# One hundred and eleven tasks at other positions in a hand-kept order of a two-stage kernel

## The chip, the cores and the metric

The kernel runs on one core of a Trainium2 chip. The core has a tensor engine (PE, with its weight loads listed as PEld), a vector engine (DVE), a scalar engine (ACT), GpSimd (POOL, idle here) and a sync engine (SP) that issues the DMAs. Each engine takes its own instructions in order, and semaphores hold an instruction until what it needs is there. The metric is the device time of one execution in microseconds (us).

## The reference

Attention with positive random features over 8 batches, 8 heads, 576 tokens and a head width of 64, and then a feed-forward layer with the activation g = h tanh(softplus(h)) on the 4608 tokens of width 512:

```python
def phi(x):
    proj = np.einsum('bhsd,df->bhsf', x, w_phi)                  # 64 -> 128 features
    proj = proj - np.max(np.abs(proj), axis=-1, keepdims=True)
    return np.concatenate([np.exp(proj), np.exp(-proj)], axis=-1)
q_p, k_p = phi(q), phi(k)
kv  = np.einsum('bhsf,bhsd->bhfd', k_p, v)
z   = np.sum(k_p, axis=2)
num = np.einsum('bhsf,bhfd->bhsd', q_p, kv)
den = np.einsum('bhsf,bhf->bhs', q_p, z)[..., None] + 1e-06
x   = (num / den)            # transposed to 4608 x 512
h   = x @ w_in               # 512 -> 2048
sp  = np.where(h > 20.0, h, np.log1p(np.exp(np.minimum(h, 20.0))))
out = (h * np.tanh(sp)) @ w_out                                  # 2048 -> 512
```

## The kernel before

All work is cut into 3160 small tasks, each on one engine with a name, and the names are used in this document.

Attention. "project k15" or "project q5_0" multiplies 512 columns of keys or queries by w_phi into two PSUM banks, pp0 and pp1 (eight matmuls, in turn to pp0 and pp1, line 422). "centre" on DVE takes the largest magnitude of each (line 426) and subtracts it (line 434): up to k16 and q5_1 one task of four instructions (maximum of pp0, maximum of pp1, subtraction of pp0, subtraction of pp1), later four tasks, "max" and "centre" with 0 and 1. "exp" on ACT makes both exponentials. "sum k15 13" adds a block of keys into the product with v of pair 13 in PSUM, "kv 13" copies it out (on DVE or ACT), "num q5_0 0" multiplies queries by it, "divide" on DVE divides by the denominator, and the result is turned (by PE early, by a DMA round trip with "regroup" on DVE later) and split into a high and a low part ("high", "low").

Feed-forward. A chunk c has 256 tokens; "in c f" multiplies its x by 128 columns of w_in (12 matmuls of fp32r: high by high, high by low, low by high, line 660) into half of a PSUM bank h; when both halves (f even and f odd) are there, "mish" on ACT reads the bank. "out c f" multiplies by w_out (lines 695 and 830). From chunk 4 on, "mix", "mixh", "mixl" build sums of the activations and the out products run on sums of weights (tasks "wsum", "comb", "combh", "combl", "send", made once, between about 180 and 300 us) with seven instead of eight products. The weights themselves are split into two parts early, by "abs", "clamp", "shift", "sign", "rest", "power", "split" and "ready".

Banks. PSUM has three pools: "att" with four buffers, "h" with two and "o" with two. The bank of "in c f" is of pool "h". From k15 on, a projection's pp0 is of pool "h" too and its pp1 of pool "att". A new tile waits until the last reader of the tile that had its buffer is done.

Order. `Plan.order` is a list scheduler with due times. Its result goes through `relinked`, which moves single tasks on their engine's own line by the list MOVES: a pair (name, ahead) puts the task directly ahead of another one on the same engine. The lines of the four engines are then merged into one program order by needs. What stands first on an engine is done first there; a task that waits holds up all behind it.

Of the kernel before, what the change touches and what calls it, by code (L numbers as in the profile page):

```python
# [87 lines left out]
BURST = ("share", "sum", "num", "project")  # L88
PATIENCE = 1.451

MOVES = (("rest ('in', 2, 2)", "low 1 2"), ("low 1 1", "sign ('in', 2, 1)"),
# [7 lines left out]


def relinked(tasks):

    by_name = {task["name"]: task for task in tasks}
    line, at = {}, {task["name"]: n for n, task in enumerate(tasks)}
    for task in tasks:
        line.setdefault(task["engine"], []).append(task["name"])
    for name, ahead in MOVES:
        own = line[by_name[name]["engine"]]
        own.remove(name)
        own.insert(own.index(ahead), name)  # L110
    needs, then, key = dict.fromkeys(at, 0), {name: [] for name in at}, {}
    for task in tasks:
        for need in {*task["deps"], *task["after"]}:
            needs[task["name"]] += 1
            then[need].append(task["name"])
    for own in line.values():
        first = len(tasks)
        for one, two in zip(own, own[1:]):
            needs[two] += 1
            then[one].append(two)  # L120
        for name in reversed(own):
            first = key[name] = min(first, at[name])
    heap = sorted((key[name], at[name], name) for name in at if not needs[name])
    order = []
    while heap:
        name = heapq.heappop(heap)[2]
        order.append(by_name[name])
        for other in then[name]:
            needs[other] -= 1
            if not needs[other]:  # L130
                heapq.heappush(heap, (key[other], at[other], other))
    return order


class Plan:
# [11 lines left out]
    def order(self):  # L147
# [5 lines left out]
        done, slots, released, freed = {}, {}, {}, {}  # L153
# [27 lines left out]
        while any(waiting.values()):  # L181
            moved = False
            for engine, queue in waiting.items():
                if free[engine] > now or not queue:
                    continue
                found, held = None, engine == "PE" and last["kind"] in BURST and now > 190
                line = queue[:48]
# [39 lines left out]
                moved = True  # L227
# [5 lines left out]
        tasks = [task for _, _, task in issued]  # L233
        at = [n for n, task in enumerate(tasks) if task["name"].startswith("load ")][:NLOADS]
# [3 lines left out]
        moved = [next(task for task in tasks if task["name"] == name) for name in LATER]  # L238
        tasks = [task for task in tasks if task["name"] not in LATER]
        at = 1 + next(n for n, task in enumerate(tasks) if task["name"] == LATER_THAN)  # L240
        return relinked(tasks[:at] + moved + tasks[at:])


@with_exitstack
def attention_then_mish(ctx, tc, qT, kT, va, w_phi, w_in, w_out, out):
# [842 lines left out]
    def plan_fast(n, c, m):  # L1088
# [13 lines left out]
        for order, i in enumerate(by_use):  # L1102
            nth, kind = 4 * late + i, "kept" if i == 4 else "late" if c == NCH - 1 and late >= 0 else "ring"
            if kind == "kept" and c > FAST:
                continue
            if kind == "ring" and c > FAST and place < 2:
                ends.append(loaded[m % 2, i][1])
                continue
            r = 4 * (m % 2) + i if i < 4 else NFT // 2 + m
            slot, token, after = f"hs{r}", f"hs:{key} {i}", []  # L1110
            deps = [plain_out(FAST - 1, r), f"wsum {r // 2} {r % 2}"]
            if kind == "ring":
                if (m % 2, i) in loaded:
                    deps, after = [], [loaded[m % 2, i][0]]
                loaded[m % 2, i] = f"term {key} {i}", token
                if c == NCH - 1 or place < NFT // 2 - 2:
                    ends.append(token)
            elif kind == "late":
                slot, token, deps = "e", f"late:{nth // 2}", []
                after = [f"term {key} {i ^ 1}"] if i in (0, 2) else []  # L1120
            add(f"term {key} {i}", "SP", n + 0.5 + LAGF - TLEAD + 0.1 * order, 0.42, lambda i=i: load_term(c, m, i),
                deps=deps + [f"send {m} {min(i // 2, 2)} {p}" for p in range(2)], size=262144, after=after,
                take=([] if kind == "late" and i in (0, 2) else [(slot, token)]) + [("flight", f"flight:{key} {i}")],
                give=[f"flight:{key} {i}"])
            uses.append(f"term {key} {i}")
# [143 lines left out]
```

## Time and profile before

| | |
|---|---|
| runs | 1037.94, 1039.55, 1039.72 us; median 1039.55 |
| the profiled execution | 1039.22 us, its span 1037.4 us |
| granted TensorE clock, mean | 0.998 |
| PE / DVE / ACT busy | 1024.1 / 737.4 / 652.4 us |
| DMA | 223.09 MB, mean 215 GB/s |

The span is the time from the first to the last instruction; around it lie 1.8 us. A row of the timeline has the start, how long the group of like instructions ran, the engine, the line, the operation, the tiles (out<-in), shapes and count, and in brackets the idle time before it and what ended that. Matmuls are pipelined: the ends of two of them overlap, so the time from one start to the next start says more than the length. fp32 matmuls have two records each.

### The profile page before, as it was taken

To read this page: it belongs to the slowest core of one execution; us is meant where nothing else is said; L and a number is where in the kernel's file an instruction comes from. 1 tells how busy PE (TensorE), PEld (TensorE's weight loads), DVE (VectorE), ACT (ScalarE), POOL (GpSimd) and SP (SyncE) were. 2 spreads that over 40 slices of the span, in tenths; PEclk is the share of its full clock that TensorE was granted. 3 is DMA by queue.
4 is the path that set the end of the run, shared out by engine and by line. 5 is a ranking of instruction groups with operands and counts; after the bars stand their busy time and mean duration, and the time that the engine had idled before them with its cause. 6 is when DMAs were issued, how large, how long until landed. Compare 5 with 4: busy or idle time off the path is not lost.

```text
span 1037.4 us, 30074 instructions
## 1 busy us (share of the span) xinstructions
PE 1024.1 (99%) x12286; PEld 985.0 (95%) x12286; DVE 737.4 (71%) x1692; ACT 652.4 (63%) x1026; POOL 0.7 (0%) x6
## 2 busy tenths in 40 slices
PE   8999999999999999999999999999999999999998
PEld 7888998899889999999999999999999999999998
DVE  7998998677877676767676767675776766666553
ACT  6689897667665756666666656655666565545532
POOL 0000000000000000000000000000000000000000
PEclk9999999999999999999999999999999999999999
DMA  9879564465977666767667564857576666775844
GB/s 321 278 246 311 176 212 141 126 201 165 289 250 231 218 208 203 237 208 236 210 208 242 188 206 162 258 178 247 175 229 209 213 184 215 223 221 184 288 150 156
DMA packets 158313, 223.09 MB, mean 215 GB/s; under 512 B 17120, under 2 KB 75616, under 8 KB 158176
## 3 DMA queue, kind: packets, MB, share of 16 engines
q1 hardware_dynamic: 158032, 221.11, 65.6%
q8 instruction: 97, 1.59, 0.7%
q14 instruction: 40, 0.33, 0.1%
q10 hardware_dynamic: 144, 0.07, 0.0%
HBM read 177.59 MB, written 43.52 MB: 213 GB/s over the span
## 4 chain that ended last, share of the span: by engine, by line
PE 90%; ACT 3%; DMA 3%; DVE 2%; issue 1%; SPq 0%; ACTq 0%; DVEq 0%
PE h L660 37%; PE oy L830 8%; PE o L695 8%; PE ox L830 7%; PE ow L830 7%; PE num L463 6%; PE kvps L463 6%; PE oz L830 4%; PE pp_q L422 4%; PE pp_k L422 3%; DMA v<-va 1%; DMA terms<-comb 1%; DMA middle_out<-w_out 1%; PE kvps L527 0%; ACT e_k L448 0%
## 5 line engine op out<-in xcount | busy, mean ns | idle before, releaser
L660 PE MATMUL h<-xTh,win 128*128 128x256 f32 x2304 | 429.4, 281 | 1.0 <-DVE e_k L434 1.0
L660 PEld LDWEIGHTS h<-xTh,win 128*128 128x128 f32 x2304 | 360.8, 188 | 5.1 <-PE h L660 1.2
L660 PE MATMUL h<-xTl,win 128*128 128x256 f32 x1152 | 321.6, 279 | 0.0
L660 PEld LDWEIGHTS h<-xTl,win 128*128 128x128 f32 x1152 | 216.6, 188 | 1.7
L745 DVE TENSOR_TENSOR sl<-s,sh 128x640 fp32r<-128x640 f32 x112 | 91.9, 821 | 106.0 <-ACT sh L741 101.5
L741 ACT CAST sh<-s 128x640 fp32r<-128x640 f32 x112 | 80.6, 722 | 89.8 <-DVE s L736 80.4
L726 ACT ACTIVATE u<-h 128x512 f32<-128x512 f32 x112 | 66.8, 597 | 94.1 <-PE h L660 93.6
L734 DVE TENSOR_TENSOR s<-u 128x256 f32<-128x256 f32 x112 | 46.8, 418 | 90.6 <-ACT u L726 90.4
L830 PE MATMUL oy<-wout,sh 128*128 128x256 f32 x448 | 85.1, 283 | 0.0
L830 PE MATMUL ox<-wout,gh 128*128 128x256 f32 x440 | 82.7, 281 | 0.0
L830 PE MATMUL ow<-wout,sh 128*128 128x256 f32 x440 | 82.1, 279 | 0.0
L695 PE MATMUL o<-wout,gh 128*128 128x512 f32 x256 | 81.4, 399 | 0.0
L463 PE MATMUL num<-kv,e_q 128*64 128x66 f32 x2304 | 77.6, 225 | 1.5 <-DVE xTl L644 1.0
L463 PE MATMUL kvps<-v,e_k 128*64 128x66 f32 x2272 | 75.6, 223 | 2.7 <-issue 2.0
L463 PEld LDWEIGHTS kvps<-v,e_k 128*64 128x64 f32 x2272 | 70.0, 137 | 8.4 <-issue 3.7
L463 PEld LDWEIGHTS num<-kv,e_q 128*64 128x64 f32 x2304 | 72.8, 139 | 4.3 <-DVE xTl L644 1.2
L498 ACT ACT_TABLE_LOAD x25 | 32.1, 1283 | 63.7 <-DVE e_k L434 63.3
L830 PEld LDWEIGHTS oy<-wout,sh 128*128 128x128 f32 x448 | 68.3, 188 | 1.6
L830 PEld LDWEIGHTS ox<-wout,gh 128*128 128x128 f32 x440 | 67.1, 188 | 0.7
L830 PEld LDWEIGHTS ow<-wout,sh 128*128 128x128 f32 x440 | 66.9, 188 | 0.0
L830 PE MATMUL oy<-wout,sl 128*128 128x256 f32 x224 | 62.7, 280 | 0.0
L830 PE MATMUL ox<-wout,gl 128*128 128x256 f32 x220 | 61.5, 280 | 0.0
(122 smaller groups left out, 1834.1 us busy)
## 6 DMA issues: line engine op xcount, KB each, us to landing
wout<-terms SPq DMA_DIRECT2D x344, 256.0 KB, 4.5
there_e<-e_q SPq DMA_DIRECT2D x60, 256.0 KB, 2.7
e_q<-there_e SPq DMA_DIRECT2D x240, 64.0 KB, 2.3
v<-va SPq DMA_DIRECT2D x32, 330.0 KB, 4.5
out<-osb SPq DMA_DIRECT2D x35, 256.0 KB, 2.6
raw_k<-kT SPq DMA_DIRECT2D x34, 256.0 KB, 3.5
raw_q<-qT SPq DMA_DIRECT2D x34, 256.0 KB, 3.5
there_x<-via SPq DMA_DIRECT2D x30, 256.0 KB, 2.0
```

Of the source, the lines that this page charges most:

```text
L422: nc.tensor.matmul(ps[j][:, n], raw[rows, n * P:(n + 1) * P], w_phi2[rows], start=True, stop=True)
L463: nc.tensor.matmul(ps[rows], lhsT[h], rhs[h], start=start, stop=stop, skip_group_check=True)
L498: nc.scalar.activation(e[:, 1, :], e[:, 0, :], AF.Exp)
L660: nc.tensor.matmul(ps, w[:, wcol], x[:, cc % 2, :], start=(n == 0), stop=(n == 11))
L695: nc.tensor.matmul(ps.rearrange("p (k n) -> p k n", k=2), g[:, cols], w, start=(i == first and k == 0), stop=(i == end and k == 2))
L726: nc.scalar.activation(u, h_live.pop((c, fp)).rearrange("p f s -> p (f s)"), AF.Mish)
L734: nc.vector.tensor_tensor(s[:, :CH], u[:, :CH], u[:, CH:], op=ALU.add)
L741: nc.scalar.copy(mix_high[c, fp], mixed[c, fp])
L745: nc.vector.tensor_sub(mix_low[c, fp], mixed.pop((c, fp)), mix_high[c, fp].bitcast(F32))
L830: nc.tensor.matmul(ps, a, b, start=(begins and n == 0 and (apart or not half)), stop=(ends and n == 2), skip_group_check=True)
```

## The change

111 pairs are added to the 18 of MOVES. Tasks between 39 and 360 us and in two stretches near 630 and 740 us get other places on PE, ACT and DVE; the order of SP stays as it was. `relinked` now also gives each task the sorted places of its engine's line when it merges the lines, and keeps a list of held buffers: a task that would take a buffer of a full pool is set back until one is given up. The work itself is the same. On PE, the pairs that the prediction speaks of are these:

```diff
+UNBUFFERED = ("flight", "mix", "prep", "w")
+
 MOVES = (("rest ('in', 2, 2)", "low 1 2"), ("low 1 1", "sign ('in', 2, 1)"),
...
+         ("in 1 3", "project k7"), ("split ('in', 1, 2)", "evict 0 7 0"), ("abs ('in', 0, 1)", "abs ('out', 0, 0)"),
...
+         ("num q5_0 1", "sum k15 13"), ("clamp ('out', 12, 0)", "rest ('out', 13, 0)"),
...
+         ("combh 7 1", "mish 4 0"), ("in 4 1", "out 3 15"), ("out 3 6", "out 3 8"), ("in 3 11", "out 3 8"),
...
-def relinked(tasks):
+def relinked(tasks, ring_of, limits):
...
+    for own in line.values():
+        for place, name in zip(sorted(at[name] for name in own), own):
+            at[name] = place
...
+        for ring, token in task["take"]:
+            if ring not in UNBUFFERED:
+                rings.setdefault(token, set()).add(ring_of(ring, token))
...
-        name = heapq.heappop(heap)[2]
-        order.append(by_name[name])
+        entry = heapq.heappop(heap)
+        task = by_name[entry[2]]
+        taken = [(ring_of(ring, token), token) for ring, token in task["take"] if ring not in UNBUFFERED]
+        taken = [(ring, token) for ring, token in taken if token not in held.setdefault(ring, set())]
+        if any(len(held[ring]) + sum(r == ring for r, _ in taken) > limits.get(ring, 1) for ring, _ in taken):
+            kept.append(entry)
+            continue
+        order.append(task)
```

The first place is PE around project k15, at 265 to 272 us. Before, the end of project q5_0 is followed by the out product 3 6 and by in 3 11, the second half of bank h_3_10:

```order
L422 MATMUL pp0_q5_0_3980<-w_phi2_98,raw_q5_0_3820 128x128
L422 MATMUL pp1_q5_0_3981<-w_phi2_98,raw_q5_0_3820 128x128
L695 MATMUL o_3_0_0_3637<-wout_6_0_1602,gh0_3_3_3802 128x512 x2
L695 MATMUL o_3_0_0_3637<-wout_6_0_1602,gl0_3_3_3814 128x512
L695 MATMUL o_3_0_1_3638<-wout_6_0_1602,gh0_3_3_3802 128x512 x2
L695 MATMUL o_3_0_1_3638<-wout_6_0_1602,gl0_3_3_3814 128x512
L660 MATMUL h_3_10_3853<-xTh_3_0_3074,win_0_2_1964 128x256
L660 MATMUL h_3_10_3853<-xTl_3_0_3082,win_0_2_1964 128x256
```

Now the same end of project q5_0 is followed by project k15:

```order
L487 MATMUL pp0_q5_0_3976<-w_phi2_98,raw_q5_0_3820 128x128
L487 MATMUL pp1_q5_0_3977<-w_phi2_98,raw_q5_0_3820 128x128
L487 MATMUL pp0_k15_4006<-w_phi2_98,raw_k15_3812 128x128 [waits DMAHW7_49,DVE_49,PE_49]
L487 MATMUL pp1_k15_4007<-w_phi2_98,raw_k15_3812 128x128
L487 MATMUL pp0_k15_4006<-w_phi2_98,raw_k15_3812 128x128
L487 MATMUL pp1_k15_4007<-w_phi2_98,raw_k15_3812 128x128
```

Project k15 has moved ahead of out 3 6, in 3 11 and out 3 7; its first matmul waits for a DMA (its keys), for DVE and for PE. In the same way project k17 now stands directly behind project q6_0 (it stood behind out 4 2), and project k18 directly behind project q6_1 (it stood behind in 5 13 and out 4 6).

The second place is PE at 291 to 296 us. Before, project k16 follows project q5_1; the rows are the last of q5_1 and the first of k16:

```order
L422 MATMUL pp0_q5_1_4382<-w_phi2_98,raw_q5_1_4209 128x128
L422 MATMUL pp1_q5_1_4383<-w_phi2_98,raw_q5_1_4209 128x128
L422 MATMUL pp0_k16_4398<-w_phi2_98,raw_k16_4205 128x128 [waits DMAHW2_49,Activation_49]
L422 MATMUL pp1_k16_4399<-w_phi2_98,raw_k16_4205 128x128 [waits DVE_49]
L422 MATMUL pp0_k16_4398<-w_phi2_98,raw_k16_4205 128x128
```

Now project q5_1 follows project k16:

```order
L487 MATMUL pp0_k16_4357<-w_phi2_98,raw_k16_4205 128x128
L487 MATMUL pp1_k16_4358<-w_phi2_98,raw_k16_4205 128x128
L487 MATMUL pp0_q5_1_4388<-w_phi2_98,raw_q5_1_4209 128x128 [waits DMAHW3_49,DVE_49,PE_49]
L487 MATMUL pp1_q5_1_4389<-w_phi2_98,raw_q5_1_4209 128x128
L487 MATMUL pp0_q5_1_4388<-w_phi2_98,raw_q5_1_4209 128x128
```

The two projections have changed places, and the second of them, which waited for ACT before, now waits for DVE. num q5_0 1 stands ahead of sum k15 13, and in 4 1, which stood ahead of out 3 13, behind project q5_1.

The third place is DVE at the same time. Before, kv 14 and the two divides of q5_0 are followed by the combined weights 7 and by the centre of q5_1; the centre of k16 stands eight rows further on:

```order
L556 COPY kv_14_4374<-kvps_14_4321 128x264 [waits PE_49]
L608 TENSOR_SCALAR r0_5_0_4378<-num0_5_0_4336 128x4 [waits PE_49]
L609 RECIPROCAL r0_5_0_4378<-r0_5_0_4378 128x4 [waits DVE_49]
L610 TENSOR_TENSOR x_5_0_4377<-num0_5_0_4336,r0_5_0_4378 128x256 [waits DVE_49]
L608 TENSOR_SCALAR r1_5_0_4392<-num1_5_0_4357 128x4 [waits PE_49]
L609 RECIPROCAL r1_5_0_4392<-r1_5_0_4392 128x4 [waits DVE_49]
L610 TENSOR_TENSOR x_5_0_4377<-num1_5_0_4357,r1_5_0_4392 128x256 [waits DVE_49]
L766 TENSOR_TENSOR comb1_7_4396<-wsum0_7_4260,wsum1_7_4264 128x512 [waits DMAHW3_49]
L768 TENSOR_TENSOR comb2_7_4408<-wsum0_7_4260,wsum1_7_4264 128x256 [waits DMAHW5_49]
L426 TENSOR_REDUCE m0_q5_1_4412<-pp0_q5_1_4382 128x4 [waits PE_49]
```

Now kv 14 is followed by comb 7 0, kv 13, a divide, combl 7 0 and a divide, and then by the centre of k16:

```order
L829 TENSOR_TENSOR comb0_7_4351<-wsum1_7_4258 128x256 [waits DVE_49]
L615 TENSOR_TENSOR kv_13_3946<-kvps_13_4291,kv_13_3946 128x264
L673 TENSOR_SCALAR r0_5_0_4368<-num0_5_0_4334 128x4 [waits PE_49]
L674 RECIPROCAL r0_5_0_4368<-r0_5_0_4368 128x4 [waits DVE_49]
L675 TENSOR_TENSOR x_5_0_4367<-num0_5_0_4334,r0_5_0_4368 128x256 [waits DVE_49]
L843 TENSOR_TENSOR comb0_7_4351<-comb0_7_4351,combh0_7_4354 128x512 [waits Activation_49]
L673 TENSOR_SCALAR r1_5_0_4376<-num1_5_0_4262 128x4
L674 RECIPROCAL r1_5_0_4376<-r1_5_0_4376 128x4 [waits DVE_49]
L675 TENSOR_TENSOR x_5_0_4367<-num1_5_0_4262,r1_5_0_4376 128x256 [waits DVE_49]
L491 TENSOR_REDUCE m0_k16_4380<-pp0_k16_4357 128x4 [waits PE_49]
L491 TENSOR_REDUCE m1_k16_4382<-pp1_k16_4358 128x4 [waits PE_49]
L499 TENSOR_TENSOR e0_k16_4384<-pp0_k16_4357,m0_k16_4380 128x512 [waits DVE_49]
```

The centre of k16 has moved ahead of comb 7 1 and of the centre of q5_1, and comb 7 0, kv 13 and combl 7 0 have moved in between kv 14 and it.

## Rows read from the trace of the kernel before

**Rows 1.** the page: busy times; ACT's busy tenths in 40 slices

```profile
PE 1024.1 (99%) x12286; PEld 985.0 (95%) x12286; DVE 737.4 (71%) x1692; ACT 652.4 (63%) x1026; POOL 0.7 (0%) x6
...
ACT  6689897667665756666666656655666565545532
```

**Rows 2.** the timeline of all engines around project k15 (start, length, engine)

```profile
265.49 1.16 PE L422 MATMUL pp_q<-w_phi,raw_q 64*128 64x128 f32 x16
...
266.58 0.73 PE L695 MATMUL o<-wout,gh 128*128 128x512 f32 x2
...
267.17 1.28 DVE L426 TENSOR_REDUCE m_q<-pp_q 128x4 f32<-128x512 f32 x2
...
268.37 1.28 DVE L434 TENSOR_TENSOR e_q<-pp_q,m_q 128x512 f32<-128x512 f32 x2
```

**Rows 3.** the timeline of all engines around projects q5_1 and k16

```profile
290.94 2.04 PE L463 MATMUL num<-kv,e_q 128*64 128x66 f32 x64
291.44 0.76 DVE L764 TENSOR_TENSOR comb<-wsum 128x256 f32<-128x256 f32 x2 [3.71 <-DMA terms<-comb]
...
292.88 0.69 DVE L778 TENSOR_TENSOR comb<-comb,combh 128x512 fp32r<-128x512 f32 x1
...
292.91 0.48 PE L422 MATMUL pp_q<-w_phi,raw_q 64*128 64x128 f32 x2
...
293.84 0.42 DVE L556 COPY kv<-kvps 128x264 f32<-128x264 f32 x1
...
294.18 0.15 DVE L608 TENSOR_SCALAR r<-num 128x4 f32<-128x4 f32 x1
...
295.65 0.68 DVE L766 TENSOR_TENSOR comb<-wsum,wsum 128x512 f32<-128x512 f32 x1
...
295.95 0.73 PE L695 MATMUL o<-wout,gh 128*128 128x512 f32 x2
...
302.82 0.36 PE L660 MATMUL h<-xTh,win 128*128 128x256 f32 x1 [1.01 <-DVE e_k L434]
```

**Rows 4.** the timeline of all engines around project q6_0

```profile
326.81 1.29 DVE L426 TENSOR_REDUCE m_q<-pp_q 128x4 f32<-128x512 f32 x2 [0.23 <-PE pp_q L422]
...
326.82 0.50 PE L830 MATMUL oy<-wout,sh 128*128 128x256 f32 x2
...
328.02 1.28 DVE L434 TENSOR_TENSOR e_q<-pp_q,m_q 128x512 f32<-128x512 f32 x2
```

**Rows 5.** the timeline of all engines around project q6_1

```profile
351.65 0.38 PE L660 MATMUL h<-xTh,win 128*128 128x256 f32 x1
...
351.84 0.68 DVE L426 TENSOR_REDUCE m_q<-pp_q 128x4 f32<-128x512 f32 x1
```

**Rows 6.** the timeline of PE around in 10 4

```profile
627.58 1.11 PE L463 MATMUL num<-kv,e_q 128*64 128x66 f32 x32
...
630.21 1.16 PE L463 MATMUL num<-kv,e_q 128*64 128x66 f32 x32
631.30 1.16 PE L422 MATMUL pp_q<-w_phi,raw_q 64*128 64x128 f32 x16
```

**Rows 7.** the chain that ended last, one piece: start, length, what

```profile
362.33 5.60 PE h L660 x48
```

**Rows 8.** the timeline of all engines, 66 to 76 us

```profile
66.76 1.73 PE L422 MATMUL pp_k<-w_phi,raw_k 64*128 64x128 f32 x16
...
72.24 0.69 PE L463 MATMUL kvps<-v,e_k 128*64 128x66 f32 x16 [0.74 <-DMA v<-va]
```

**Rows 9.** the timeline of all engines around project k9

```profile
101.64 1.77 PE L422 MATMUL pp_k<-w_phi,raw_k 64*128 64x128 f32 x16
...
101.83 0.37 ACT L554 COPY kv<-kvps 128x264 f32<-128x264 f32 x1
```

**Rows 10.** by stretch: PE, PEld, DVE, ACT, POOL busy, clock, DMA

```profile
36.00:40.00 4.00, 1.78 (x18) 1.29 (x14) 3.93 (x12) 3.10 (x6) 0.00 (x0) 1.00 1.04 384
40.00:44.00 4.00, 4.00 (x66) 3.78 (x67) 3.93 (x10) 1.81 (x4) 0.00 (x0) 0.57 0.93 334
```

More of the change, by code (lines that the diff above doesn't have):

```diff
@@ L110, in relinked @@
         own.insert(own.index(ahead), name)
-    needs, then, key = dict.fromkeys(at, 0), {name: [] for name in at}, {}
+    for own in line.values():
+        for place, name in zip(sorted(at[name] for name in own), own):
+            at[name] = place
+    needs, then, key, rings, held = dict.fromkeys(at, 0), {name: [] for name in at}, {}, {}, {}
     for task in tasks:
@@ L123, in relinked @@
     heap = sorted((key[name], at[name], name) for name in at if not needs[name])
-    order = []
+    order, kept = [], []
     while heap:
-        name = heapq.heappop(heap)[2]
-        order.append(by_name[name])
-        for other in then[name]:
+        entry = heapq.heappop(heap)
[6 more added lines that the diff above has]
+        order.append(task)
+        for ring, token in taken:
+            held[ring].add(token)
+        freed = [(ring, token) for token in task["give"] for ring in rings.get(token, ()) if token in held.get(ring, ())]
+        for ring, token in freed:
+            held[ring].discard(token)
+        for other in then[entry[2]]:
             needs[other] -= 1
@@ L131, in relinked @@
                 heapq.heappush(heap, (key[other], at[other], other))
+        if freed:
+            for entry in kept:
+                heapq.heappush(heap, entry)
+            kept = []
+    if kept:
+        raise RuntimeError("no order: " + ", ".join(entry[2] for entry in kept))
     return order
@@ L240, in order @@
         at = 1 + next(n for n, task in enumerate(tasks) if task["name"] == LATER_THAN)
-        return relinked(tasks[:at] + moved + tasks[at:])
+        return relinked(tasks[:at] + moved + tasks[at:], lambda ring, token: f"part{self.place[token]}" if ring == "part" else ring,
+                        {ring: size for ring, size in self.rings.items() if ring != "part"})
 @with_exitstack
```

38 rows, old and new, of the table MOVES are left out of this document.

## The prediction

> **What bounds the kernel now.** I read the page first, then where TensorE (PE) waits, then PE and VectorE (DVE) side by side at the places that the change touches. PE is busy for 1024.1 us, 99% of the span [rows 1], so almost every microsecond that PE gains or loses is a microsecond of the kernel. It is idle for only 1037.4 - 1024.1 = 13.3 us, part of it before 61 us, where the change moves nothing on PE. What is left to win are a few short waits at 66 to 73, 101 and 292 to 303 us, and the cost of switching PE between fp32 work (project, sum, num) and fp32r work (in, out).
>
> **What the new order of PE does at four places.** A projection writes two PSUM banks, one of the pool "h" (two buffers) and one of "att". At 266 us one "h" buffer holds the half-filled h of "in 3 10", which waits for "in 3 11"; the other holds pp0 of q5_0. Before, out 3 6, in 3 11 and out 3 7 stand between project q5_0 and project k15, and in that time DVE empties pp0. After, project k15 follows project q5_0 at once, and its first matmul waits until DVE has read pp0 of q5_0. PE takes its matmuls in order, so out 3 6 and all behind it stand still. The same happens to q5_1 behind k16, to k17 behind q6_0 and to k18 behind q6_1. Each wait is worked out from the same stretch of before:
> - k15: PE is done with project q5_0 at 266.58 us. DVE reaches it at 267.17, since it is still busy with combl, kv and divide work; two maxima bring it to 268.37 and the first subtraction of 0.68 us frees pp0 at about 269.1 [rows 2]. Wait: 269.1 - 266.6 = 2.5 us. Bounds: 1.9 (an idle DVE: 0.6 + 0.6 + 0.7) to 2.8, because mish 3 4 now runs behind two casts on ScalarE (ACT) and low 3 4, ahead of the maxima on DVE, comes later.
> - q5_1: PE does sum k15 14, num q5_0 0 (half of the 1.97 us that two take) and project k16 (1.1 us), so 2.1 us lie between the end of the sums and the wait. In that time DVE must do kv 14 (0.35), comb 7 0 (0.7), kv 13 (0.35 like kv 14), a divide (0.74, half of the 1.47 between 294.18 and 295.65), combl 7 0 (0.6), a divide (0.73) and then two maxima and a subtraction (1.9): 5.4 us [rows 3]. Wait: 5.4 - 2.1 = 3.3 us; bounds 1.9 to 4.0. Two old waits go here: the two projections took 295.95 - 292.91 = 3.04 us instead of 2 x 1.09, and in 4 4 waited 1.01 us for the centre of k16 [rows 3]. In 4 4 now waits for mish 4 0, which has two matmul groups and more to run in, so nothing is late in its stead. 0.86 + 1.01 = 1.9 us are saved.
> - k17: PE leaves q6_0 at 326.82, DVE starts its maxima at once and its first subtraction ends at 328.02 + 0.68 = 328.7 [rows 4]. Wait: 1.9 us, and hardly less, since DVE was not late. Bounds 1.8 to 2.0.
> - k18: PE leaves q6_1 at 351.65. The subtraction is moved directly behind the first maximum, which runs from 351.84 to 352.5, and takes another 0.6 [rows 5]: pp0 is free at 353.1. Wait: 1.5 us. Bounds 1.3 to 1.7.
> Together 2.5 + 3.3 + 1.9 + 1.5 = 9.2 us of new waits, less 1.9 of old ones: +7.3 us. What stands behind them is all of PE's later work; after 350 us PE has no wait long enough to give any of it back.
>
> **What the change saves.** A block of "in" between two fp32 blocks is dear: num, in 10 4, num take 631.30 - 627.58 = 3.72 us, where two nums take 1.97 (290.94 to 292.91) and one "in" 1.40 (5.60 for 48 matmuls): 0.35 us for one way out and back [rows 3, 6, 7]. I take 0.30, because the nums of the two stretches have different neighbours. PE changes between the two kinds 109 times before and 97 times after, six ways out and back fewer: -1.8 us (bounds -1.2 to -2.1). Four of them go at 628 and 739 us, where "in 10 4" and "in 12 4" move behind the projections; there the bank comes free in time, since out 9 0 (2.5 us) lies between. Three go at k15, k17 and k18 and one at 180 us; two are added, where project k11 is split from q3_0 and in 1 3 put between sums.
> Early, in 1 3 and out 0 3 move into the waits around 70 us (0.74 us for v6 is the largest): from 66.76 to 72.24 PE took 5.48 us for two projections (2.2) and a sum of 48 matmul records (1.5 at the rate of 64 in 1.97), so 1.8 is the most that can be won [rows 3, 8]. But project k9 waits at 101.64 for kv 7 on ACT (1.77 us instead of 1.16), and ACT, busy for 90% or more of the slice from 78 to 104 us [rows 1], now does ready out 7 0 just ahead of kv 7 and not four tasks earlier: the sum of its work before kv 7 is the same. kv 7 stays at 101.83 and PE meets it there again [rows 9]. I take -0.3 us (bounds +0.3 to -1.8). The other moves on DVE and ACT shift tasks by about a microsecond whose results PE takes several in or out blocks (1.4 us each) later; those blocks hide them, and without that cover each would cost its 0.3 to 0.7 us.
>
> **The clock.** Between 36 and 40 us PE was busy for 1.78 of 4 us; in the next 4 us the granted clock was 0.57 in the mean, near the level of 1.2 instead of 2.4 GHz [rows 10]. PE was busy all that time, so it lost 4 x 0.43 = 1.7 us of work at full clock. The wait at q5_1 leaves PE busy for about 0.7 of 4 us, less than there, so I count one fall there: +1.7 us. At k15 PE would be busy for about 1.5 of 4 us, at k17 for 2.1: these are open.
> The Trainium skill, "TensorE: Matmul & The Clock Gate", section "HAM oscillation — how this bites in real kernels", has the clock fall again after each long idle stretch, not once; the trace agrees in that one fall. By that rule the sum would have more than one fall, 1.7 us each; rival 2 weighs that from the rows.
>
> **Sum.** +7.3 - 1.8 - 0.3 + 1.7 = +6.9 us on the profiled execution's 1039.2 us (span 1037.4 and 1.8 around it): 1046.1. That execution lies 0.3 us under the median of 1039.55 of the runs shown, so I add 0.1 here and in the rivals: 1046.2 us.
>
> **The rivals.**
> 1. The waits come, the clock holds: no fall at q5_1. 1046.2 - 1.7 = 1044.5 us. For it: the fall at 40 us came after two waits in a row, here there is one. Against it: that one leaves PE idle for longer than those two together. Chance 0.17.
> 2. The clock falls at two or three of the four places. Each further one costs 1.7: 1047.9 to 1049.6, middle 1048.8. For it: the idle share at k15 is near that of 36 to 40 us. Against it: k17 and k18 wait less. Chance 0.22. The page of the Trainium skill named above, "TensorE: Matmul & The Clock Gate", speaks for this one.
> 3. The waits are at their floors and the early gain is kept: 1.9 + 1.9 + 1.8 + 1.3 - 1.9 - 2.1 - 1.8 = +1.1, no fall: 1040.4 us. It needs kv 7 to come 1.6 us sooner on ACT, and a DVE that is never late. Chance 0.09.
> 4. On the other side: the bank is free. If the projection found an "h" buffer that ACT or DVE had emptied before, at k15, q5_1, k17 and k18, there would be no new wait at all, and only the gains stand: -1.9 (old waits) - 1.8 (switches) - 0.3 = -4.0: 1035.3 us. The point that decides is whether PE pauses after project q5_0, by more than about 1 us at each of the four places. For it: the list of moves puts the projections together in the same way at 628 and 739 us, where the bank is free. Against it: at 266 us in 3 11 is still to come, so one of the two buffers cannot be free. Chance 0.07.
>
> **Numbers.** Forecast 0.45, rivals 0.17, 0.22, 0.09, 0.07. Within 0.2% (2.1 us, about what a measurement of this kernel can tell from no change) lies rival 3: same 0.09; faster 0.07; slower 0.84. The range takes in rival 1 with smaller waits and rival 2 with the upper bounds: 1041.0 to 1050.5 us. The forecast's own range is 1044.8 to 1048.
>
> **What would show it.** In the profile after: PE idle for 2 to 3 us behind project q5_0 (near 266 us), about 3 us behind project k16 (near 295 to 298), 1.5 to 2 us behind q6_0 and q6_1, each ended by DVE's subtraction; no more wait at in 4 4; a granted clock below 1 for some microseconds after the second of these. From 360 us on the two kernels run in parallel, some 8 us apart, and at 630 and 740 us the distance shrinks by 0.6 each. If PE has no idle time between 266 and 270 us, the forecast is wrong in its main step; if it has and the time is below 1042 us, something after 360 us gave it back.

## The result, and the profile after

The changed kernel takes 1053.12 us (median of 4 runs, 1050.60 to 1053.55), the kernel before 1039.62 us beside it: 1.29% slower, ratio 1.0129 with a 95% interval of 1.0110 to 1.0148. The forecast was 1046.2 us, with a range up to 1050.5: the direction was right, but half of the loss of 13.5 us was missing.

TensorE (PE) is still what the time hangs on. It was busy for 1024.1 us before [rows 1] and is busy for 1026.0 now; the span grew by 13.7 us. From the page of the changed kernel, and then its table of PE's waits (total, times, longest):

```profile
PE 1026.0 (98%) x12286; PEld 987.6 (94%) x12286; DVE 738.8 (70%) x1692; ACT 652.7 (62%) x1026; POOL 0.7 (0%) x6
```

```profile
PE pp_k L487 <- issue: 6.0, 3, 2.4
PE pp_q L487 <- issue: 4.0, 1, 4.0
PE num L528 <- issue: 1.6, 1, 1.6
...
PE num L528 <- ACT u L791: 1.1, 1, 1.1
...
PE num L528 <- DVE x L675: 0.7, 1, 0.7
...
PE num L528 <- DVE kv L615: 0.5, 1, 0.5
```

The first two rows are the four waits that were forecast (one of the three pp_k's, one of 2.4 us, stands behind project q6_0). The last four rows were not forecast at all: the rows of 1.6, 1.1 and 0.7 us belong to the late places, the last one to num q6_0 1.

The way to find the missing time is to take the same piece of work in both traces and to subtract its start before from its start after. Only pieces ahead of which the same set of work is done will do (differences are rounded after subtraction):

| piece | start before | start after | distance | what lies between |
|---|---|---|---|---|
| num q1_0 1 | 41.94 | 40.51 | -1.43 | PE's order is the same up to here |
| in 3 3 | 241.34 | 239.99 | -1.36 | the early moves: +0.1 |
| in 5 10 | 356.81 | 367.38 | +10.57 | the four projections: +11.9 |
| out 8 3 | 549.45 | 560.08 | +10.63 | nothing |
| in 10 7 | 639.05 | 649.43 | +10.38 | four switches (two ways out and back) fewer, first place: -0.25 |
| num q11_1 0 | 653.22 | 664.76 | +11.54 | +1.2 |
| num q13_1 0 | 764.11 | 777.43 | +13.32 | +1.8 |
| out 14 6 | 899.04 | 912.66 | +13.62 | +0.3, and nothing more to the end |

**The four waits.** The timeline of PE and VectorE (DVE) around project k15 (start, length, engine, in brackets the idle time before it):

```profile
264.12 1.16 PE L487 MATMUL pp_q<-w_phi,raw_q 64*128 64x128 f32 x16
...
265.32 1.28 DVE L491 TENSOR_REDUCE m_q<-pp_q 128x4 f32<-128x512 f32 x2
...
266.52 1.28 DVE L499 TENSOR_TENSOR e_q<-pp_q,m_q 128x512 f32<-128x512 f32 x2
...
267.31 1.16 PE L487 MATMUL pp_k<-w_phi,raw_k 64*128 64x128 f32 x16 [2.02 <-issue]
```

DVE takes up the bank at 265.32, as soon as project q5_0 has ended, reads both maxima, and its first subtraction (half of the 1.28 us) ends at 267.2; project k15 starts at 267.31. Before, three pieces of out and in stood in that gap [rows 2]. The same view around project k16:

```profile
292.08 1.16 PE L487 MATMUL pp_k<-w_phi,raw_k 64*128 64x128 f32 x16
...
293.62 0.42 DVE L675 TENSOR_TENSOR x<-num,r 128x256 f32<-128x256 f32 x1
...
294.96 0.42 DVE L675 TENSOR_TENSOR x<-num,r 128x256 f32<-128x256 f32 x1
295.30 1.28 DVE L491 TENSOR_REDUCE m_k<-pp_k 128x4 f32<-128x512 f32 x2
296.50 1.28 DVE L499 TENSOR_TENSOR e_k<-pp_k,m_k 128x512 f32<-128x512 f32 x2
...
297.28 2.08 PE L487 MATMUL pp_q<-w_phi,raw_q 64*128 64x128 f32 x16 [4.04 <-issue]
```

Here DVE is late. Project k16 ends at 293.24, but DVE does a divide, a low part of comb and another divide before it turns to the maxima at 295.30: 2.1 us of queue on top of 1.9 us of reading, 4.04 us together. Project q5_1 then takes 2.08 us where 1.16 is usual: the clock is down. Around project q6_0, and at its neighbours:

```profile
330.19 1.19 PE L487 MATMUL pp_q<-w_phi,raw_q 64*128 64x128 f32 x16
...
331.18 0.71 DVE L532 STREAM_TRANSPOSE via<-x 128x512 f32<-128x512 f32 x1
331.81 1.25 DVE L491 TENSOR_REDUCE m_q<-pp_q 128x4 f32<-128x512 f32 x2
...
332.98 1.27 DVE L499 TENSOR_TENSOR e_q<-pp_q,m_q 128x512 f32<-128x512 f32 x2
...
333.76 1.78 PE L487 MATMUL pp_k<-w_phi,raw_k 64*128 64x128 f32 x16 [2.38 <-issue]
```

```profile
357.88 0.43 DVE L615 TENSOR_TENSOR kv<-kvps,kv 128x264 f32<-128x264 f32 x1
...
358.37 1.16 PE L528 MATMUL num<-kv,e_q 128*64 128x66 f32 x32 [0.48 <-DVE kv L615]
...
362.29 0.94 PE L487 MATMUL pp_k<-w_phi,raw_k 64*128 64x128 f32 x12 [1.63 <-issue]
```

The regroup of q5_1 keeps DVE until 331.8, so project k17 waits for 2.38 us. The second fence holds the wait of 1.63 us behind project q6_1 and one that nobody counted: num q6_0 1 waits 0.48 us for kv 15, which stands behind mix 5 7 on DVE, as before, and that behind ACT.

**The clock.** By stretch, the granted clock is the first of the three numbers at the end (PE's busy time is the first of the five):

```profile
36.00:40.00 4.00, 1.78 (x27) 1.34 (x26) 3.93 (x11) 3.18 (x7) 0.00 (x0) 1.00 1.05 392
40.00:44.00 4.00, 3.37 (x71) 3.23 (x68) 3.86 (x11) 2.44 (x5) 0.00 (x0) 1.00 0.86 333
296.00:300.00 4.00, 2.72 (x19) 2.52 (x20) 3.01 (x6) 0.62 (x1) 0.00 (x0) 0.57 0.47 169
300.00:304.00 4.00, 4.00 (x17) 3.62 (x17) 3.90 (x10) 1.43 (x4) 0.00 (x0) 0.58 0.25 86
332.00:336.00 4.00, 2.24 (x18) 2.05 (x19) 3.94 (x7) 0.00 (x0) 0.00 (x0) 0.76 0.20 70
336.00:340.00 4.00, 4.00 (x30) 4.00 (x29) 2.97 (x7) 0.00 (x0) 0.00 (x0) 0.81 0.16 50
```

Two stretches at half clock follow the second and the third wait. Busy time by missing clock gives 2.72 x 0.43 + 4 x 0.42 + 2.24 x 0.24 + 4 x 0.19 = 4.1 us. In 36:40 PE is busy for 1.78 us of 4, just as before [rows 10], yet 40:44 is granted 1.00 where it was 0.57.

**The late places.** Nothing was expected to wait here. The timeline around num q11_1 0 and, from another answer, around num q13_1 0:

```profile
661.87 0.71 ACT L806 CAST sh<-s 128x640 fp32r<-128x640 f32 x1
...
662.61 0.82 DVE L810 TENSOR_TENSOR sl<-s,sh 128x640 fp32r<-128x640 f32 x1 [4.49 <-ACT sh L806]
663.36 0.42 DVE L799 TENSOR_TENSOR s<-u 128x256 f32<-128x256 f32 x1
...
664.23 0.42 DVE L615 TENSOR_TENSOR kv<-kvps,kv 128x264 f32<-128x264 f32 x1
...
664.76 0.95 PE L528 MATMUL num<-kv,e_q 128*64 128x66 f32 x25 [1.07 <-ACT u L791]
```

```profile
775.05 0.60 ACT L791 ACTIVATE u<-h 128x512 f32<-128x512 f32 x1
...
775.68 0.42 DVE L799 TENSOR_TENSOR s<-u 128x256 f32<-128x256 f32 x1 [1.08 <-ACT u L791]
...
776.90 0.43 DVE L615 TENSOR_TENSOR kv<-kvps,kv 128x264 f32<-128x264 f32 x1
...
777.43 1.29 PE L528 MATMUL num<-kv,e_q 128*64 128x66 f32 x35 [1.65 <-issue]
```

Num q11_1 0 needs kv 24, DVE's addition of the sums into kv. Kv 24 could start when share k28, the last product that it needs, is through at 662.13, but it stands in DVE's queue behind mixl 10 3, which waits 4.49 us for a cast by ScalarE (ACT), and behind mix 10 4: it ends at 664.65. At 775 us it is kv 28 behind mix 12 4, which waits for ACT's mish 12 4. The third late wait, 0.69 us at 751.53 us, is num q13_0 1, which starts just after DVE's divide of q13_0 0 is done; that divide stands behind two low parts. ACT is late because in 10 4 and in 12 4 now come behind project k28 and project k32. Mish 10 2 starts at 648.23 instead of 634.10, 14.1 us later where PE's distance is 10.4, and ACT's queue hands 1.9 us of that on: exp k28 0 starts 12.3 us later (651.89 and 639.60). Another 0.95 us comes from a position of the change itself: on ACT, mish 10 4 now stands ahead of exp q11_1 0, and the cast that mixl 10 3 waits for starts 13.2 us later (661.87 and 648.63). This is read from the traces; no run moved in 10 4 or mish 10 4 back alone.

### The profile page after: what moved, and what is told of

It is laid out like the page before. It is cut to its first block, busy times and chain, and to the rows that moved or that the text cites. A ratio compares the mean times of both kernels' runs of the same rounds, so it can differ in the third digit from the quotient of the medians.

```text
span 1051.1 us, 30069 instructions
## 1 busy us (share of the span) xinstructions
PE 1026.0 (98%) x12286; PEld 987.6 (94%) x12286; DVE 738.8 (70%) x1692; ACT 652.7 (62%) x1026; POOL 0.7 (0%) x6
## 4 chain that ended last, share of the span: by engine, by line
PE 80%; DVE 6%; DMA 5%; ACT 5%; issue 2%; SPq 1%; ACTq 0%; DVEq 0%
PE h L725 33%; PE oy L895 7%; PE ox L895 7%; PE ow L895 7%; PE o L760 6%; PE num L528 5%; PE kvps L528 4%; PE oz L895 3%; PE pp_q L487 3%; PE pp_k L487 3%; DMA e_q<-there_e 1%; DMA words_in<-w_in 1%; DMA there_e<-e_q 1%; SPq L541 1%; DMA v<-va 1%
```

## The experiments

The 111 new positions fall into three groups by the start of the work before: early (up to 246 us, 53 positions), the four projections (246 to 366 us, 34), and late (620 to 770 us, 24). Every kernel below takes the changed kernel's code and only changes its table of moves. Times are medians, each beside runs of the kernel before on the same chip.

**Each group alone.**

```
early: MOVES = the 18 of before + the 53 early ones
mid:   MOVES = the 18 of before + the 34 around the four projections
late:  MOVES = the 18 of before + the 24 late ones
```

> The kernel before with only the 53 new positions of work that it starts ahead of 246 us (all three engines); nothing of 255 to 365 us and nothing of 620 to 780 us is moved. Theory A (the parts add up, each through its own waits): up to the piece in 3 3 (241 us) the changed kernel's PE was 1.36 us ahead of the kernel before, so this one ends 1.0 to 1.8 us ahead of the kernel before, near 1038.2 us, with sums k6 5 and k7 6 about 1.9 us nearer and project k9 0.7 us longer. Theory B (the early gain is only the half-clock stretch at 51 us of the record, which comes or stays away by chance): within 0.5 us of the kernel before, 1039.1 to 1040.1, with a half-clock record of 3.4 us near 40 us of the span. A loss is expected by neither.

> The kernel before with only the 34 new positions of work that it starts at 246 to 366 us (projections k15, k16, k17 and k18 next to the q projections ahead of them, and the DVE and ACT moves around them). Theory A (four pp0 waits, and the half clock that two of them bring): the PE waits behind project q5_0, project k16, project q6_0 and project q6_1 are there with 2.0, 4.0, 2.4 and 1.6 us, two half-clock stretches stand at 297 and 334 us, and from 365 us on everything is 11 to 12.5 us later than in the kernel before: 1051.0 to 1052.0 us. Theory B (the waits need the early moves, which bring other work to the same DVE at that time): the four waits together under 8 us, at most one half-clock stretch, 1045 to 1048 us.

> The kernel before with only the 24 new positions of work that it starts at 620 to 770 us. Theory A (the products with q11_1, q13_0 and q13_1 wait for DVE copies that stand in its queue behind work that ACT now hands over later): three PE waits of 1.07, 0.69 and 1.65 us behind sum k28 25, sum k31 28 and sum k32 29, less 0.2 to 0.6 for the fewer changes of number format, so 2.7 to 3.3 us slower than the kernel before: 1042.2 to 1042.9. Theory B (as in the prediction: no new wait, 1.2 us of format changes saved): 1038.3 to 1038.7. Theory C (the waits come only where the two earlier groups have shifted DMA traffic): under 0.7 us of wait, 1039 to 1039.8.

Measured: early 1037.50 us against 1039.25 before, ratio 0.9984 (0.9974 to 0.9994); mid 1048.81, 1.0093 (1.0073 to 1.0113); late 1040.90, 1.0019 (1.0008 to 1.0030).

Late bears out A in the trace: waits of 1.07, 0.57 and 1.55 us at the same three places, though nothing else was moved, and a distance that grows by 2.6 us from project k27 (604 us) to the end. By the runs it is 2.0 us (0.8 to 3.1), under A's bounds of 2.7 to 3.3, though the interval reaches them. B, the prediction's own view, and C fall.

Mid shows the four waits with 2.25, 3.44, 1.91 and 1.63 us, and two half-clock stretches, though at 268 to 272 and 299 to 303 us and none near 334. It costs 9.7 us (7.6 to 11.7); its 1048.81 us are less than A's 1051.0 to 1052.0 and more than B's 1045 to 1048. So the main part stands without the other groups, but not all of it.

Early gains 1.7 us by the runs, as A has it. Its trace says otherwise: at num q1_0 1, ahead of every move on PE, it is already 1.98 us ahead of the profile of before, and at in 1 12 (214 us) 2.07. From 42 us to 214 us the early moves are worth 0.1 us in that profile.

**The same kernel again.**

```
after_again: MOVES as in the changed kernel
```

> The changed kernel once more, on the chip of the runs beside it. Theory A (the three groups add up, as their own runs gave on another chip: -1.7, +9.6 and +1.7 us): 9 to 10.5 us over the kernel before. Theory B (the groups need one another: the first result of +13.5 us holds on any chip): 12.5 to 14.5 us over the kernel before.

1052.55 us against 1039.11, ratio 1.0129 (1.0111 to 1.0146), +13.4 us: B. The groups alone come to -1.7 + 9.7 + 2.0 = 10.0. The difference of 3.4 us is only just clear of the intervals (about 2.6 us either way on the sum, 1.8 on this run). Most of it shows in one place of the traces: from num q5_1 1 to in 4 13, around project k17, the distance grows by 3.2 us in the first profile of the changed kernel, by 4.4 in this one, and by 1.6 in mid. The idle times there hardly differ (2.38 us; 0.26 and 1.80; 0.13 and 1.91). The clock does: it falls in both profiles of the changed kernel and not in mid. This run's stretches, in part:

```profile
264.00:268.00 4.00, 1.98 (x27) 1.70 (x24) 4.00 (x8) 0.00 (x0) 0.00 (x0) 0.95 0.70 244
268.00:272.00 4.00, 4.00 (x18) 3.42 (x18) 3.82 (x8) 0.00 (x0) 0.00 (x0) 0.62 0.12 19
332.00:336.00 4.00, 2.91 (x20) 2.72 (x21) 3.59 (x7) 0.00 (x0) 0.00 (x0) 0.56 0.19 70
336.00:340.00 4.00, 4.00 (x23) 4.00 (x23) 2.65 (x6) 0.00 (x0) 0.00 (x0) 0.59 0.21 56
```

PE's busy time in 264:268 is 1.98 us here and in the first profile, and so are its waits (2.02 us each). Here 268:272 is granted 0.62, there 1.00.

**DVE turns to the bank first.**

```
 MOVES = (..., ("project q14_0", "out 12 2"),
+         ("centre k16 0", "divide q5_0 0"),
+         ("regroup q5_1", "regroup q6_0 0"),
+         ("centre q6_0 0", "max q6_0 1"))
```

> The changed kernel with three more positions on DVE alone: centre k16 0 ahead of divide q5_0 0 (it stood behind both divides and a low part), and max and centre of q6_0, first half first, ahead of regroup q5_1. TensorE's order is the changed kernel's. Theory A (TensorE waits for DVE's reading of the first bank and for what stands ahead of it in DVE's queue, and the half clock follows on the length of the wait): the wait behind project k16 falls from 4.04 us to 2.0 to 2.4, that behind project q6_0 from 2.39 to 1.3 to 1.6, the half-clock stretches at 297 and 334 us go or get shorter: 1046 to 1049 us. Theory B (same waits, but the clock falls whatever their length): waits as in A, both stretches still there, 1049.9 to 1050.4. Theory C (the wait is for the loads of k16 and k17 or for another engine): waits unchanged, 1052.5 to 1053.5.

1048.06 us, ratio 1.0086 (1.0067 to 1.0105) to its kernel before: +8.9 us where the changed kernel has +13.4. PE's timeline at the two places, with one row of DVE's at the second:

```profile
297.05 1.16 PE L572 MATMUL pp_q<-w_phi,raw_q 64*128 64x128 f32 x16 [2.40 <-issue]
...
330.66 0.69 DVE L584 TENSOR_TENSOR e_q<-pp_q,m_q 128x512 f32<-128x512 f32 x1
...
331.45 1.16 PE L572 MATMUL pp_k<-w_phi,raw_k 64*128 64x128 f32 x16 [1.52 <-issue]
```

The waits are 2.40 and 1.52 us: A, to its numbers. PE's order was not touched, so the length of these waits is set by DVE's queue; C falls. At the second place DVE now subtracts the first bank before it reads the second: project k17 starts 0.1 us after that first subtraction (330.66 + 0.69), so it is the first bank, pp0, that it waits for. For the clock it is neither A nor B. Behind the two shortened waits one stretch is shorter and one is gone, but the clock now falls behind the first and the fourth wait as well, which are as long as they were (2.02 and 1.62 us):

```profile
268.00:272.00 4.00, 4.00 (x20) 3.25 (x18) 4.00 (x9) 0.00 (x0) 0.00 (x0) 0.61 0.05 17
360.00:364.00 4.00, 4.00 (x23) 4.00 (x23) 2.73 (x7) 1.00 (x2) 0.00 (x0) 0.59 0.58 199
```

**Other work in the four gaps.**

```
 MOVES = (..., ("project q14_0", "out 12 2"),
+         ("out 3 6", "project k15"), ("out 3 7", "project k15"),
+         ("out 3 15", "project q5_1"), ("out 4 2", "project k17"),
+         ("out 4 6", "project k18"))
```

> The changed kernel with five pieces of TensorE's order moved into its four waits: out 3 6 and out 3 7 between project q5_0 and project k15, out 3 15 between project k16 and project q5_1, out 4 2 between project q6_0 and project k17, out 4 6 between project q6_1 and project k18; DVE and ACT keep the changed kernel's order. Theory A (only the bank that DVE still reads holds the second projection, and other products could run in that time): the waits of 2.0, 4.0, 2.4 and 1.6 us fall to under 0.2, 1.0 to 1.6, under 0.2 and under 0.2, the half clock near 300 and 335 us goes, and up to 1.2 us go for four more pairs of format changes: 9 to 12 us faster than the changed kernel. Theory B (the wait moves on, since DVE is what these 100 us are bound by): 1 to 4 us faster, with new waits of 1.5 to 3 us at the pieces that follow each second projection. Theory C (as A, but the half clock comes whatever fills the gap, at the changes of format): 7 to 8.5 us faster.

1040.86 us (the median of nine runs, 1040.24 to 1042.18; a tenth run took 2544 us, which stays unexplained), ratio 1.0019 (1.0008 to 1.0030) to before. Against the changed kernel beside it that is 11.7 us faster, in the upper part of A's range; B and C fall. Three of the four waits are gone, the one at project q5_1 is 0.46 us (the second row below), the clock is full from 250 to 370 us, and what is left is small; from its table of PE's waits:

```profile
PE h L812 <- ACT u L878: 0.7, 1, 0.7
...
PE pp_q L574 <- PE o L847: 0.5, 1, 0.5
```

So five moves of PE's out pieces, with every other move in place, undo 11.7 of 13.4 us.

**One gap left open.**

```
 the five moves of filled, without ("out 3 15", "project q5_1")
```

> As filled, with one of the four gaps left open: out 3 15 stands behind in 4 1 again, so project q5_1 follows project k16 directly; the other three stay filled. Theory A (each gap costs its wait and the half clock behind it, whatever the others do): a wait of 3.4 to 4.0 us at project q5_1 and a half-clock stretch of 3.4 to 6.8 us behind it, 4.5 to 6.6 us slower than filled. Theory B (the half clock comes only when several waits follow each other): the wait alone, 3.0 to 4.0 us slower than filled, full clock throughout.

1043.18 us, ratio 1.0037 (1.0023 to 1.0052): 1.9 us slower than filled by the ratios to before (about 0.1 to 3.7 with both intervals), 2.7 by the differences of medians. Neither theory gave the size: A's 4.5 us and more are out, B's 3.0 to 4.0 are not excluded by the runs, but its full clock is by the trace. The wait is there with 3.44 us, and so is one half-clock stretch, of which this row holds the second part:

```profile
296.00:300.00 4.00, 4.00 (x21) 3.68 (x21) 4.00 (x8) 1.31 (x3) 0.00 (x0) 0.76 0.19 66
```

From in 4 2 on onegap is 3.8 us later than filled, less than wait and clock together, since filled has small waits there itself. Then it gets some back: project q6_0 takes 2.03 us in filled (0.46 idle) and 1.12 here, and at 621 us out 9 1 takes 3.41 us in filled (0.60 of it waiting for a DMA of weights) and 2.55 here. So 2.0 us are left at 626 us, and 2.4 at the last projections. In these two traces a gap alone gives part of its cost back at later waits; that the next gap gave nothing back in the changed kernel is a reading that no run tests.

**The late group mended.**

```
late2: MOVES = late's
+         ("kv 24", "mixl 10 3"), ("kv 28", "mix 12 4"),
+         ("divide q13_0 0", "low 12 1")
```

> The kernel before with the late group's 24 new positions and three more on DVE: kv 24 ahead of mixl 10 3, kv 28 ahead of mix 12 4, divide q13_0 0 ahead of low 12 1. Theory A (the three late waits are DVE's queue: the copy of the sums stands behind mix and low parts that wait for ACT): the waits of 1.07, 0.57 and 1.55 us go to under 0.2 each, so 2.6 to 3.0 us faster than the late group alone and 0.2 to 1.0 us faster than the kernel before. Theory B (another need of num q11_1 0 and num q13_1 0, the exponentials of ACT, ends the wait at nearly the same time): the waits keep 0.7 us or more, 0.5 to 1.5 us slower than the kernel before.

1039.53 us, ratio 1.0002 (0.9991 to 1.0013), against late's 1.0019: 1.8 us of 2.0 are gone. The three waits are under 0.2 us, as A said, but A's other half, a kernel faster than the one before, did not come: there are two new waits of 0.45 and 0.34 us and one of 0.26 at project k33, since the copies behind kv 24 and kv 28 are now the ones that stand behind mix; DVE and PE around num q11_1:

```profile
651.11 0.43 DVE L613 TENSOR_TENSOR kv<-kvps,kv 128x264 f32<-128x264 f32 x1 [4.02 <-PE kvps L590]
...
653.52 0.43 DVE L619 COPY kv<-kvps 128x264 f32<-128x264 f32 x1
...
654.00 1.16 PE L526 MATMUL num<-kv,e_q 128*64 128x66 f32 x32 [0.45 <-DVE kv L619]
```

So the late group, even mended, wins nothing that can be measured.

**Looking for a version that beats both.**

```
early_late2:  early's and late2's positions
early_again:  early's
early_kv7:    early's without ("ready ('out', 7, 0)", "kv 7") on ACT
early_filled: early's, mid's and the five moves of filled
```

> The early group's 53 positions and the late group's 24 with the three DVE positions of the run before, none of the group around the four projections: a version that may beat both kernels. Theory A (groups add up): -1.7 of the early group and -0.2 to -1.0 of the mended late one, 1.7 to 2.8 us faster than the kernel before. Theory B (the early group's -1.7 us were the chance of the start-up and of the half clock at 40 us): within 0.6 us of late2.

> The early group alone once more, beside the kernels that build on it. Theory A (its first result of -1.7 us holds): 1.0 to 2.2 us faster than the kernel before. Theory B (what its trace shows from 60 to 245 us, about 0.8 us won at sums k6 5 and k7 6 and as much lost at project k9 and project q3_1, is all there is, and the rest was the chance of the start-up): within 0.7 us of the kernel before.

> The early group without its one ACT position that puts ready ('out', 7, 0) directly ahead of kv 7. Theory A (project k9 waits for ACT's kv 7, and that one piece of 0.6 us ahead of it makes the wait longer): the wait of 0.81 us falls to 0.2 to 0.3, and the time by 0.5 to 0.6 us against the early group alone. Theory B (kv 7 waits for TensorE's sum k8 7 or stands behind mish 1 2 anyway): the wait stays over 0.6 us and the time within 0.2 us.

> The early group and the group around the four projections with its four gaps filled as in the run filled, without the late group. Theory A (late costs what its own trace showed, 2.9 us, less the 1.2 us that runs did not confirm): 1.7 to 2.9 us faster than filled, so 0.3 to 1.0 us faster than the kernel before. Theory B (the filled gaps keep 1 us of waits of their own and the early group gives nothing): within 0.3 us of the kernel before or slower.

Early_late2: 1038.80 us, ratio 1.0002 (0.9992 to 1.0012), the same ratio as late2: B, no gain shown. Early_again: 1038.09 against 1038.76, 0.9990 (0.9979 to 1.0000): 0.7 us by medians, 1.0 by the ratio, on the edge between A and B. Early_filled: 1038.39, 0.9998 (0.9989 to 1.0007): no difference shown from the kernel before; by the ratios 2.2 us (0.21%) better than filled, near the late group's cost once more, as A had it. A's other half, 0.3 to 1.0 us under the kernel before, is not shown, and B's bound of 0.3 us fits as well.

Early_kv7: 1037.63, 0.9991 (0.9981 to 1.0001). Theory A fell: the wait at project k9 stayed at 0.82 us. ACT and PE at that place:

```profile
97.37 1.28 ACT L754 ACT_TABLE_LOAD   x1
98.66 0.60 ACT L754 ACTIVATE u<-h 128x512 f32<-128x512 f32 x1
...
99.91 0.37 ACT L642 COPY kv<-kvps 128x264 f32<-128x264 f32 x1
...
100.33 1.16 PE L510 MATMUL pp_k<-w_phi,raw_k 64*128 64x128 f32 x14 [0.82 <-ACT kv L642]
```

Kv 7 comes behind mish 1 2, which follows a table load of 1.28 us; the piece taken out from between only moved to the front of the same queue. So what the early moves win at 72 us is lost at project k9 because ACT's chain ends when it ends.

The early group is the best version found: 0.9984, 0.9990 and, but for one position, 0.9991, so 0.9 to 1.7 us under the kernel before, with intervals of which two reach no difference. The others show no gain over it.

## Why the prediction was half right

**The four waits: right.** Forecast 2.5, 3.3, 1.9 and 1.5 us; measured 2.02, 4.04, 2.38 and 1.63: 10.1 instead of 9.2. At k15 DVE was not busy with earlier work, as the forecast of 2.5 had it, but free at 265.32. Dvefirst and filled show the cause as the prediction put it: the bank that DVE still reads. K17's bounds (1.8 to 2.0) were too narrow, for "DVE was not late" was read from before, where the regroup of q5_1 was done in time. After, PE came through num q5_1 and project q6_0 while that regroup still ran.

**A wait at num q6_0 1: missed**, 0.5 us. The old waits at project q5_1 and in 4 4 went, as forecast.

**The clock: mis-sized.** One fall of 1.7 us was counted; two came, one of them twice as long, 4.1 us by the stretches. This is rival 2's size for this term, with its mechanism. The Trainium skill, "TensorE: Matmul & The Clock Gate", section "HAM oscillation — how this bites in real kernels", has the clock go down again with each long idle stretch rather than once; these traces agree that it falls more than once, but not that each wait brings a fall: of four waits two did in the first profile of the changed kernel, those two and a third (at project k15) in the second. Rival 1 (no fall) and rival 4 (a free bank, no waits) are out, and so is rival 3.

**The step that failed: the late places.** The prediction put "-1.2 us" there (four of its six round trips between fp32 and fp32r) and let the rest be hidden: "The other moves on DVE and ACT shift tasks by about a microsecond whose results PE takes several in or out blocks (1.4 us each) later; those blocks hide them". The bank did come free in time behind out 9 0, as it said. But in 10 4 feeds ACT, ACT feeds DVE, and kv 24 stands in DVE's queue behind what ACT hands over. Measured: +3.0 us (10.57 to 13.62), from three waits of 3.4 us, less 0.25 and about 0.4 us for the round trips, half of what was put for them, and 0.3 us after 777 us whose cause is not known. This term is off by 4.2 us, the largest of all. Late reproduced its waits alone; late2 took them away with three moves on DVE, though smaller ones came in their place.

**The early moves: right in the profile**, -0.3 forecast, +0.1 measured between 42 and 241 us. That they are given back at project k9 was right too; the reason given, ready out 7 0 ahead of kv 7, was wrong (early_kv7).

**The start: not in the sum.** Before its first moved piece on PE the changed kernel's profile was already 1.4 us ahead, of which the missing half-clock stretch at 40 us is a part. This is the chance of one execution, as the last section's starts show, and it hid as much of the loss from the profile's balance.

By stages, then: start 0 forecast, -1.4 measured; early -0.3 (0.0 with its switches, one way out and back saved and two added, 0.3 each) and +0.1; projections +8.1 (9.2 - 1.9 + 1.7 - 0.9 for three round trips) and +11.9; late -1.2 and +3.0. The prediction's last test, parallel from 360 us and 0.6 us less at 630 and 740 each, is what the table of distances refutes.

That the early group gains 1.0 to 1.7 us by the runs and 0.1 by the profile is explained in part only. The half clock at 40 us stands in 5 of 10 profiles with the early order and in 3 of 4 without. Each run's mean granted clock says more: it is 0.997 or 0.998, as in the profiles whose one fall is the one at 40 us, in 17 of 69 runs with the early order (the early kernels and filled) and in 57 of 105 without (the kernel before, late, late2; two runs at 0.949 are left out). Runs of the kernel before with such a clock are 1.2 us longer in the median than those above it (1039.42 and 1038.19), so the rarer fall gives about 0.4 us, an estimate from these numbers. The rest is open, and so is why the early order meets the fall less often. Why the clock falls near 334 us in the changed kernel and not in mid is open as well.

## What to carry to other kernels

Where a product's result must be read out before its bank can be used again, put other products into that time: five pieces moved into four gaps were worth 11.7 of 13.4 us, while a reader that came sooner was worth 4.5. When a producer is moved later, follow its result through every queue it passes, to the small copy at the end that the next product waits for, and not only to the next engine. And compare the start of like pieces in two traces before any stage is blamed: a distance table finds the stages in minutes, and shows what the start-up alone has done.

## What the hardware did that I had not expected

With one and the same order of PE up to 60 us, the clock at 40 us fell in some profiles and not in others, with PE busy for 1.78 us of 36:40 in the kernel before and in the changed one; only the former fell. Behind the wait of 2.02 us at project k15 it fell in after_again and dvefirst, not in the first profile of the changed kernel. By the rows of its stretches a fall cost 1.3 to 2.9 us. A single profile thus tells that a wait can bring the half clock, not that it will.

The first 45 us differed by up to 2.6 us between profiles in which PE does the same work in the same order there: num q1_0 1 starts at 41.94 us in the kernel before, at 39.94 in late, at 39.34 in early_again. That is more than two of the three groups are worth.
